# The head of an attention and feed-forward kernel: key copies from separate PSUM tiles, an earlier values' matrix, and two softmax tiles turned by DMA

## The chip, the cores and the metric

The kernel runs on one core of a Trainium2 chip. The time is the device time of the whole program in microseconds (us), the median of three runs. A profile of one execution shows each engine's instructions: TensorE (PE, with its weight loads as PEld), VectorE (DVE), ScalarE (ACT), GpSimd (POOL) and the queue of SyncE (SP), which here only issues DMAs.

## The reference

Attention in which each block of 96 positions looks at one sorted block, and behind it a gated feed-forward layer. 4 batches, 8 heads, 768 positions of 64 elements, 8 blocks a head; 3072 tokens of 512 elements go through w_in (512 x 2048) and w_out (2048 x 512).

```python
P = sort_net                                  # (4, 8, 8, 8)
for _ in range(5):                            # Sinkhorn
    P = exp(P - P.max(-1)); P = P / (P.sum(-1) + 1e-9); P = P / (P.sum(-2) + 1e-9)
k_sorted = einsum('bhij,bhjcd->bhicd', P, k in blocks)
v_sorted = einsum('bhij,bhjcd->bhicd', P, v in blocks)
scores = q_block @ k_sorted_block.T / sqrt(64)      # 96 x 96 per block and head
attn = softmax(scores)
x = (attn @ v_sorted_block), heads side by side     # (3072, 512)
h = x @ w_in
out = (h * cos(h)) @ w_out
```

## The kernel before

The tokens are done in eight chunks n = 0 to 7 of 384 tokens: chunk n is batch n // 2 and four of its eight blocks. A unit u = 0 to 3 of a chunk is one block with its eight heads. Within each engine the instructions run in the order in which the program text issues them (it is written out by hand, lines 900 to 1221); engines wait for each other through semaphores that the framework derives from the tiles that are read and written. Two engines that use the same bank of one PSUM tile are put one after the other by it. PSUM has two pools: `big`, three tiles of two banks, called B in the hand-written order, and `acc`, two tiles of one bank, called C.

The head is what comes before the feed-forward products of chunk 0. Its steps:

- `sort_net` (8 KB) is loaded on SP's queue. POOL issues all other loads: queries, keys and values of batch 0, the four parts of w_in, the queries of chunk 1, the four parts of w_out, and later the next batch. POOL's loads go through one DMA queue (q0 in the profile), SP's DMAs through another (q1).
- VectorE sets constants and zeros (lines 231 to 239), then runs Sinkhorn with ScalarE's exponentials (lines 302 to 376).
- `block` (line 380) multiplies selection matrices with the sorted P; `spread` (line 391), on VectorE, puts the result on the diagonal blocks of `bds[0]` (keys) or `bdv` (values).
- `kp` (line 744) multiplies 16 slices of the keys with the block matrix into a PSUM tile of two banks; `k_place` copies half the blocks of such a tile to kT, the first half (half 0) for chunk 0, the second for chunk 1. There are three such tiles, 0, 1 and 2, and the copies are shared between VectorE (V) and ScalarE (A).
- POOL permutes half of the values (`v_permute`, line 169); `v0` (line 774) multiplies eight slices of the values with bdv; `v0e` copies them to vS on ScalarE. vS has a column of ones per block, set by `ones` on POOL, so that the product with it gives the softmax's sums.
- For each unit of chunk 0, in the order 0, 3, 1, 2: `s_ps` (line 791) makes the scores; `s_max` and `s_sub` on VectorE take the maximum and subtract it; `expo` (line 565) makes the exponential on ScalarE into one of three buffers p_buf, 96 x 8 x 128 with 32 columns of padding a head; the tile is turned to pT; `av_products` multiplies it with vS, `av_norm` divides on VectorE; `x_ps` turns the result on TensorE and `x_ev` copies it to xT.
- The turning has two ways. With `on_pe` true, `p_ps` transposes the eight heads on TensorE into PSUM and `p_ev` copies them to pT on VectorE or ScalarE. Otherwise `expo` itself issues a DMA transpose of the whole p_buf, padding included, on SP's queue (line 588). In the head all four units are turned on TensorE; from chunk 2 on most are turned by DMA. The buffer of unit 0 is used again by the fourth exponential, that of unit 2.
- `keep_warm` (line 244) issues products of a tile of zeros whose result is overwritten. In the head there are ten between the scores and the av products, through the argument `fill`.
- From `up_four` on (line 850) the products with w_in and w_out follow, with the work of chunk 1 between them. `z_vperm`, `z_turned` and `p_pads` are POOL's zeros; `p_pads` sets the padding of the three p_bufs for the DMA transposes of the later chunks.

Of the kernel before, what the change touches and what calls it, by code (L numbers as in the profile page):

```python
# [10 lines left out]
FP32 = mybir.dt.float32  # L11
# [7 lines left out]
def kernel(  # L19
# [15 lines left out]
    nc = tc.nc  # L35
    B, H, S, D = q.shape
    nb = sort_net.shape[-1]
    blk = S // nb
# [9 lines left out]
    IC = 4  # L48
# [5 lines left out]
    NB = H2 * nb  # L54
# [40 lines left out]
    vS = {}  # L95
# [107 lines left out]
    PB = H * nb  # L203
# [5 lines left out]
    pick, pick_pair = pick_at(0, 2), pick_at(2, 2)  # L209
# [16 lines left out]
    def ones(g):  # L226
        nc.gpsimd.memset(vS[g][:, :, D:D + 1], 1.0)
# [10 lines left out]
    nc.vector.memset(nones[:], 0.0)  # L238
    zero_words(nc.vector, vperm[64:, CD - 12 * blk:CD])

    early = const.tile([128, 1], FP32, name="early")
    nc.scalar.activation(early[:], half_pi[:], AF.Exp)

    def keep_warm(times, t, cols=512):
        for _ in range(times):
            nc.tensor.matmul(
                t[:, :cols], warm[:], warm[:, :1].to_broadcast([128, cols]),
                start=True, stop=True)
# [131 lines left out]
    def block(picked, pool=acc, tag="acc"):  # L380

        ps = pool.tile([128, nb], FP32, name="bl", tag=tag)
        for z, part in enumerate(picked):
            n = part.shape[2]
            for j in range(nb):
                nc.tensor.matmul(
                    ps[z * n:(z + 1) * n], part[:, j], sorted_by[:, :, j],
                    start=(j == 0), stop=(j == nb - 1))
        return ps

    def spread(dst, ps, rows=slice(0, 128), xs=slice(0, 2 * H)):
        shape = [rows.stop - rows.start, xs.stop - xs.start, nb]
        nc.vector.tensor_tensor(
            dst[rows, xs], maskp[rows, xs].to_broadcast(shape),
            ps[rows].unsqueeze(1).to_broadcast(shape), op=ALU.mult)

    blocks = [block([pick[:]])]
    spread(bds[0], blocks[0], xs=slice(H, 2 * H))

    def values_matrix():  # L400
        spread(bdv, blocks[1], xs=slice(0, H))
        spread(bds[0], blocks[0], xs=slice(0, H))
        spread(bdv, blocks[1], xs=slice(H, 2 * H))

    MH = H2 * IC

    def k_products(ps, t, c, rows, rhs, keys=kbuf):
        nc.tensor.matmul(  # L408
            ps[:, t], keys[rows, c * 2 * D:(c + 1) * 2 * D], rhs, start=True, stop=True)
# [155 lines left out]
    def expo(n, u, on_pe=False):  # L565
        p = p_bufs[cnt[0] % NP]
        cnt[0] += 1


        nc.scalar.activation(  # L570
            p[:, :, :blk], s_t.pop((n, u)).rearrange("p e h c -> p (e h) c"), AF.Exp,
            scale=scale)
        if u == 0 and n in (NQ, NQ + 1):

            w = 2 * H2 * blk
            c = 2 * (QZ + D) + (n - NQ) * w
            t = kbuf[:, c:c + w].rearrange("p (a c) -> p a c", c=blk)
        elif n < LATE:
            t = ptp.tile([128, 2 * H2, blk], BF16, name="pT", tag="pT")
        else:  # L580

            z, w = (n * IC + u) % 8, 2 * H2 * blk
            t = vperm[:, z * w:(z + 1) * w].rearrange("p (a c) -> p a c", c=blk)
        pT[n, u] = t
        if on_pe:
            pb[n, u] = p
        else:
            nc.sync.dma_start_transpose(out=t[:], in_=p.rearrange("p a c -> p (a c)"))
# [25 lines left out]
    def av_products(n, u, fill=0):  # L614
        g, b2, ih = where(n)
        if n not in xT:
            xT[n] = xtp.tile([128, KC, TC], BF16, name="xT", tag="xT")
        a = big.tile([128, 2, 512], FP32, name="av", tag="big")
        keep_warm(fill, a[:, 0], 256)
        pt = pT.pop((n, u)).rearrange("p a c -> p (a c)")  # L620
        for hp in range(2):
            for h2 in range(H2):
                e = hp * H2 + h2
                w = 128 if e < 2 * H2 - 1 else blk
                nc.tensor.matmul(  # L625
                    a[:w, hp, h2 * (D + 1):(h2 + 1) * (D + 1)],
                    pt[:blk, e * blk:e * blk + w],
                    vS[g][:, v_at(g, b2, hp, h2, ih * IC + u), :D + 1],
                    start=True, stop=True)
        av_ps[n, u] = a  # L630
# [104 lines left out]
    def z_vperm():  # L735
        nc.gpsimd.memset(vperm[:64, :VN * blk], 0.0)

    def p_pads():
        for t in p_bufs:
            nc.gpsimd.memset(t[:, :, blk:], 0.0)  # L740

    ps = {}

    def kp(t, pool, tag, fill=0):
        o = ps["k", t] = pool.tile([128, 16, 2 * NB], FP32, name="ks", tag=tag)
        keep_warm(fill, o[:, :8].rearrange("p t n -> p (t n)"))
        for z in range(16):
            k_products(o, z, t * 16 + z, slice(0, 128),
                       bds[0][:, H:].rearrange("p x i -> p (x i)"))

    def k_place(t, eng, half=None):
        lo, hi = (0, nb) if half is None else (half * IC, half * IC + IC)
        o = ps["k", t]
        copy_on(
            eng, kT[0].rearrange("p z (h i) t -> p z h i t", i=nb)[
                :, ::2, :, lo:hi, t * 16:t * 16 + 16],
            o.rearrange("p t (e h i) -> p e h i t", e=2, i=nb)[:, :, :, lo:hi])

    def kxp(t):
# [14 lines left out]
    def v0(z, pool, tag, fill=0):  # L774
        o = ps["v", z] = pool.tile([128, 8, 2 * NB], FP32, name="vs", tag=tag)
        keep_warm(fill, o.rearrange("p t n -> p (t n)"))
        for t in range(8):

            d = z * 8 + t
            w = 1 if d >= VN else min(8 - t, 2)  # L780
            m = blk if d >= VN and t == 7 else 128
            nc.tensor.matmul(  # L782
                o[:m, t:t + w].rearrange("p w n -> p (w n)"), v_cols(d, d >= VN, m),
                bdv[:, :H].rearrange("p x i -> p (x i)").unsqueeze(1).to_broadcast(
                    [128, w, 2 * NB]), start=True, stop=True)
# [5 lines left out]
    def s_ps(n, u, fill=0):  # L791
        o = ps["s", n, u] = big.tile([128, 2, 512], FP32, name="sc", tag="big")
        keep_warm(fill, o[:, 0])
        if n == 0:
            for a in range(2 * H2):
                hp, c = a // H2, (u * H2 + a % H2) * blk
                for x in range(2):
                    rows = slice(x * D, (x + 1) * D)
                    m, w = a % H2 * nb + u, HT if a % H2 == H2 - 1 else 64
                    keys = kT[0][rows, 2 * hp].rearrange("p m t -> p (m t)")  # L800
                    nc.tensor.matmul(
                        o[:, x, a * HT:a * HT + w], q_of(0, hp)[rows, c:c + 128],
                        keys[:, m * HT:m * HT + w], start=True, stop=True)
            return
        if u < 2:
            by_half(n, u, o)
            return
        for h2 in range(H2):
            for hp in range(2):
                scores(o[:, hp, h2 * 128:h2 * 128 + blk], n, u, h2, hp)  # L810
# [86 lines left out]
    def w_next(eng=A, pool=None, tag="acc"):  # L897
        v_sort_g(next(wz), 4, eng, pool or acc, tag)

    kp(2, *B)  # L900
    kp(0, *B)
    v_permute(slice(0, 64), 32, False, 8, 40)
    v_permute(slice(0, 64), 40, False, 8, 48)
    v_permute(slice(0, 64), 48, False, 8, 56)
    v_permute(slice(0, 64), 56, False, 8, 64)
    k_place(2, A, 1)
    k_place(2, V, 0)
    kp(1, *B)
    k_place(0, A, 0)
    blocks.append(block([pick[:, :, z * PB:(z + 1) * PB] for z in (1, 0)]))  # L910
    k_place(1, V, 0)
    k_place(1, A, 1)
    values_matrix()
    k_place(0, A, 1)
    s_ps(0, 0, fill=3)
    v0(4, *C)
    s_max(0, 0)
    v0(0, *B)
    v0e(4, A)
# [9 lines left out]
    load_w_out(2)  # L929
    load_w_out(3)  # L930
    v0(6, *C)
    ones(0)
    expo(0, 0, True)
    s_ps(0, 2)
    s_sub(0, 3)
    v0(1, *C)
    v0e(6, A)
    s_max(0, 1)
    expo(0, 3, True)
    v0(3, *B, fill=2)  # L940
    s_sub(0, 1)
    v0e(1, A)
    p_ps(0, 0, *C, fill=2)
    v0e(3, A)
    s_max(0, 2)
    v0(7, *C)
    expo(0, 1, True)
    kxp(2)
    v0(2, *B, fill=1)
    p_ev(0, 0, V)  # L950
    v0e(7, A)
    s_sub(0, 2)
    kxp(0)
    p_ps(0, 1, *C)
    v0e(2, A)
    p_ps(0, 3, *C)
    p_ev(0, 1, V)
    expo(0, 2, True)
    kxp(1)
# [1 line left out]
    z_turned(1)  # L961
    av_norm(0, 0, True)
    av_products(0, 1)
    p_ev(0, 3, A)
    p_ps(0, 2, *C)
    av_norm(0, 1, True)
    x_ps(0, 0, *B)
# [1 line left out]
    p_ev(0, 2, A)  # L969
    load(vbuf, 64, vin_d[1])  # L970
    picks(pick_pair, (2, 3))
    av_products(0, 3, fill=2)
    av_norm(0, 3, True)
    x_ps(0, 1, *C)
    x_ev(0, 0, A)
# [12 lines left out]
    up_four(0, 3, 1)  # L988
    z_turned(0)
    cos_four(0, 0)  # L990
    p_pads()
    up_four(0, 1, 0)
    cos_four(0, 3)
    gate_four(0, 0)
# [256 lines left out]
```

## Time and profile before

| | |
|---|---|
| runs | 232.80, 232.88, 232.88 us; median 232.88 |
| profiled execution, first to last instruction | 231.6 us |
| TensorE busy | 223.5 us, 97% |
| VectorE, ScalarE, POOL busy | 170.9, 154.2 and 95.9 us |
| first product with w_in (line 857) | starts at 27.86 us |

The profile's own time is the span; the difference to the runs' median lies before the first and after the last instruction. A line of a timeline or a group names the start and the time in us, the engine, the line of the program, the operation, output<-inputs by tile name, the shapes, the count, and in brackets the idle time before it with the engine that ended it. Where a helper issues the instruction the line is the helper's: line 257 is every copy on ScalarE, 259 every copy on VectorE. A row of a DMA queue gives packets, megabytes and the packets' time as a share of 16 engines; a row of DMA issues gives their count, size and the median time from issue to landing.

### The profile page before, as it was taken

What the parts mean: (1) busy time and instruction counts of PE and PEld (TensorE: products, weight loads), DVE (VectorE), ACT (ScalarE), POOL (GpSimd) and SP (SyncE); (2) the same over time, 40 slices, a digit from 0 to 9 for tenths busy, and PEclk for the clock granted to TensorE, in tenths of its full rate; (3) what the DMA queues carried; (4) which work ended last, traced back from release to release, by engine and by line L of the source; (5) the groups of instructions that cost most, each with busy time, mean ns of one, the idle gap of its engine ahead of it and who ended that gap; (6) DMA issues with size and microseconds to landing.
All of it is one profiled execution on the core that took longest, in us unless ns stands there. A gap on an engine that the chain in (4) does not pass through costs nothing.

```text
span 231.6 us, 5534 instructions
## 1 busy us (share of the span) xinstructions
PE 223.5 (97%) x2268; PEld 138.9 (60%) x2268; DVE 170.9 (74%) x291; ACT 154.2 (67%) x207; POOL 95.9 (41%) x121
## 2 busy tenths in 40 slices
PE   8888999999999999999999999999999999999994
PEld 3477898567665566644666456555655566556553
DVE  6769968978789778877389986997699769745700
ACT  5658877777789858794888566746675666716521
POOL 7999999399950188932709000900000000000000
PEclk9999999999999999999999999999999999999999
DMA  5999999994999999797989839964923450351012
GB/s 69 230 191 207 202 207 233 199 225 139 125 135 172 174 137 148 130 168 158 154 138 89 122 72 146 215 90 92 207 91 69 90 167 0 68 146 45 0 45 93
DMA packets 67673, 31.21 MB, mean 135 GB/s; under 512 B 56384, under 2 KB 63168, under 8 KB 67392
## 3 DMA queue, kind: packets, MB, share of 16 engines
q0 software_dynamic: 24048, 13.64, 43.5%
q1 hardware_dynamic: 43312, 17.02, 35.1%
q8 instruction: 18, 0.29, 0.5%
q10 hardware_dynamic: 288, 0.20, 0.3%
q14 instruction: 7, 0.06, 0.1%
HBM read 27.27 MB, written 6.29 MB: 145 GB/s over the span
## 4 chain that ended last, share of the span: by engine, by line
PE 85%; DMA 5%; DVE 3%; POOL 2%; ACT 2%; issue 1%; SPq 1%; POOLq 0%; ACTq 0%
PE h L669 30%; PE o L694 28%; PE h L857 5%; PE o L878 5%; DMA kTs<-kTs 4%; PE av L625 3%; PE sc L438 3%; PE ks L408 2%; PE o L1215 2%; PE pps L835 1%; PE xps L656 1%; PE sc L504 1%; PE vs L782 1%; PE xps L844 1%; SPq L421 1%
## 5 line engine op out<-in xcount | busy, mean ns | idle before, releaser
L669 PE MATMUL h<-xT,w_in_t 128*128 128x384 bf16 x448 | 78.4, 326 | 0.0
L694 PE MATMUL o<-w_out_t,gg 128*128 128x512 bf16 x320 | 76.2, 379 | 0.0
L677 DVE TENSOR_TENSOR gg<-c,h 128x768 bf16<-128x768 f32 x56 | 52.7, 949 | 20.0 <-ACT c L673 20.0
L673 ACT ACTIVATE c<-h,half_pi 128x768 f32<-128x768 f32 x56 | 50.4, 900 | 25.3 <-PE h L669 24.4
L669 PEld LDWEIGHTS <-w_in_t 128*128 128x128 bf16 x448 | 42.2, 98 | 26.5 <-DMA xT<-xn 0.4
L694 PEld LDWEIGHTS <-gg 128*128 128x128 bf16 x320 | 28.9, 98 | 28.4
L179 POOL COPY vperm<-kv 64x768 bf16<-64x768 bf16 (+2 forms) x12 | 28.4, 2413 | 3.9 <-DMA kv<-in_v_dram 3.9
L570 ACT ACTIVATE p_buf<-s 96x768 bf16<-96x768 f32 x32 | 26.6, 842 | 5.1 <-DVE s L491 4.0
L489 DVE TENSOR_REDUCE mx<-sc 96x4 f32<-96x384 f32 (+1 forms) x33 | 24.0, 728 | 2.2 <-PE sc L504 2.2
L491 DVE TENSOR_TENSOR s<-sc,mx 96x384 f32<-96x384 f32 (+1 forms) x33 | 24.3, 735 | 1.6
L638 DVE TENSOR_TENSOR xn<-av,r 96x512 bf16<-96x512 f32 x32 | 22.0, 686 | 1.1
L129 POOL DMA_DIRECT2D kv<-in_q_dram x24 | 16.0, 680 | 0.8 <-issue 0.5
L257 ACT COPY kv<-o 128x512 f32<-128x512 f32 (+2 forms) x10 | 5.2, 523 | 14.1 <-PE o L694 11.5
L257 ACT CAST kTs<-ks 128x512 bf16<-128x512 f32 (+1 forms) x18 | 11.0, 630 | 5.3 <-PE ks L408 4.4
L636 DVE RECIPROCAL r<-av 96x8 f32<-96x8 f32 x32 | 6.4, 199 | 7.9 <-PE av L625 7.6
L878 PE MATMUL o<-w_out_t,gg 128*128 128x512 bf16 x48 | 11.7, 379 | 0.0
L438 PE MATMUL sc<-kTs,q_turned 128*128 128x96 bf16 x152 | 11.0, 206 | 0.5 <-DMA kTs<-kTs 0.5
L129 POOL DMA_DIRECT2D q_mem<-in_q_dram x16 | 10.7, 690 | 1.8 <-DMA kv<-in_v_dram 1.5
L259 DVE COPY kv<-o 128x512 f32<-128x512 f32 (+1 forms) x5 | 3.1, 612 | 11.1 <-PE o L1215 8.5
L857 PE MATMUL h<-xT,w_in_t 128*128 128x192 bf16 x128 | 11.1, 246 | 0.0
L438 PEld LDWEIGHTS <-q_turned 128*128 128x128 bf16 x152 | 8.8, 98 | 3.0 <-issue 0.6
L857 PEld LDWEIGHTS <-w_in_t 128*128 128x128 bf16 x128 | 10.5, 98 | 0.0
(134 smaller groups left out, 279.1 us busy)
## 6 DMA issues: line engine op xcount, KB each, us to landing
out_dram<-kv SPq DMA_DIRECT2D x12, 256.0 KB, 2.6
out_dram<-o_s SPq DMA_DIRECT2D x10, 256.0 KB, 3.1
w_in_t<-in_moe_w_in_dram POOLq DMA_DIRECT2D x4, 512.0 KB, 11.8
w_out_t<-in_moe_w_out_dram POOLq DMA_DIRECT2D x4, 512.0 KB, 12.4
kv<-in_k_dram POOLq DMA_DIRECT2D x2, 768.0 KB, 9.9
kv<-in_v_dram POOLq DMA_DIRECT2D x2, 768.0 KB, 13.0
pair<-in_k_dram POOLq DMA_DIRECT2D x2, 768.0 KB, 12.4
kv<-in_v_dram POOLq DMA_DIRECT2D x6, 256.0 KB, 5.7
```

The source lines that it names most:

```text
L129: nc.gpsimd.dma_start(out=q_heads[:, i, :, e], in_=src[:, ih * IC + i, :, e])
L179: nc.gpsimd.tensor_copy(dst, src)
L438: nc.tensor.matmul(out, q_of(n, hp)[:, x:x + 128], keys_of(n, u, h2, hp), start=True, stop=True)
L489: nc.vector.reduce_max(mx[:], scv, axis=AX.X)
L491: nc.vector.tensor_tensor(s, scv, mx.to_broadcast(list(s.shape)), op=ALU.subtract)
L570: nc.scalar.activation(p[:, :, :blk], s_t.pop((n, u)).rearrange("p e h c -> p (e h) c"), AF.Exp, scale=scale)
L669: nc.tensor.matmul(h[:, f2, :w], w_in_t[:, kk, f * 128:(f + 1) * 128], xT[n][:, kk], start=(kk == 0), stop=(kk == KC - 1))
L673: nc.scalar.activation(c[:], h[:, :, :w], AF.Sin, bias=half_pi[:, 0:1])
L677: nc.vector.tensor_tensor(gt[n, fp // 2][:, f:f + 2], c[:], h[:, :, :w], op=ALU.mult)
L694: nc.tensor.matmul(o[:], gt[n, f // 4][:, f % 4, ts * 128:(ts + 1) * 128], w_out_t[:, f, :], start=(f == 0), stop=(f == FC - 1))
L857: nc.tensor.matmul(o[:, part, f2 * w:(f2 + 1) * w], w_in_t[:, kk, f * 128:(f + 1) * 128], xT[0][:, kk, h * w:(h + 1) * w], start=(kk == 0) ...
L878: nc.tensor.matmul(out_ps[ts][:], gt[0, q][:, f % 4, ts * 128:(ts + 1) * 128], w_out_t[:, f, :], start=(f == 0), stop=(f == FC - 1))
```

## The change

- VectorE sets the padding of the p_bufs among its first zeros; `p_pads` is gone from POOL.
- The block product of the values stands right behind that of the keys, ahead of the key products; the four spreads stand together, and the column of ones of vS[0] is set by VectorE behind them, no longer by POOL.
- `kp` takes the first slice, the number of slices, and the pool: slices 32 to 47 and 0 to 15 in tiles of `big`, 16 to 23 and 24 to 31 in two tiles of `acc`. The copies are: 32 first half VectorE, 0 first half ScalarE, 16 both halves VectorE, 24 both halves ScalarE; the second halves of 0 and 32 follow on ScalarE behind the first scores and the first value products.
- Units 0 and 3 are turned by the DMA transpose that `expo` issues; their `p_ps` and `p_ev` are gone. Units 1 and 2 stay on TensorE.
- The ten products of zeros are gone.

```diff
+    for t in p_bufs:
+        nc.vector.memset(t[:, :, blk:], 0.0)
...
-    blocks = [block([pick[:]])]
+    blocks = [block([pick[:]]), block([pick[:, :, z * PB:(z + 1) * PB] for z in (1, 0)])]
     spread(bds[0], blocks[0], xs=slice(H, 2 * H))
-
-    def values_matrix():
-        spread(bdv, blocks[1], xs=slice(0, H))
-        spread(bds[0], blocks[0], xs=slice(0, H))
-        spread(bdv, blocks[1], xs=slice(H, 2 * H))
+    spread(bdv, blocks[1], xs=slice(0, H))
+    spread(bds[0], blocks[0], xs=slice(0, H))
+    spread(bdv, blocks[1], xs=slice(H, 2 * H))
+    nc.vector.memset(vS[0][:, :, D:D + 1], 1.0)
...
-    def p_pads():
-        for t in p_bufs:
-            nc.gpsimd.memset(t[:, :, blk:], 0.0)
...
-    def kp(t, pool, tag, fill=0):
-        o = ps["k", t] = pool.tile([128, 16, 2 * NB], FP32, name="ks", tag=tag)
-        keep_warm(fill, o[:, :8].rearrange("p t n -> p (t n)"))
-        for z in range(16):
-            k_products(o, z, t * 16 + z, slice(0, 128),
+    def kp(c, n, pool, tag):
+        o = ps["k", c] = pool.tile([128, n, 2 * NB], FP32, name="ks", tag=tag)
+        for z in range(n):
+            k_products(o, z, c + z, slice(0, 128),
                        bds[0][:, H:].rearrange("p x i -> p (x i)"))
...
-    kp(2, *B)
-    kp(0, *B)
+    kp(32, 16, *B)
+    kp(0, 16, *B)
+    kp(16, 8, *C)
+    kp(24, 8, *C)
     v_permute(slice(0, 64), 32, False, 8, 40)
...
-    k_place(2, A, 1)
-    k_place(2, V, 0)
-    kp(1, *B)
+    k_place(32, V, 0)
     k_place(0, A, 0)
-    blocks.append(block([pick[:, :, z * PB:(z + 1) * PB] for z in (1, 0)]))
-    k_place(1, V, 0)
-    k_place(1, A, 1)
-    values_matrix()
+    k_place(16, V, 0)
+    k_place(24, A, 0)
+    k_place(16, V, 1)
+    k_place(24, A, 1)
+    s_ps(0, 0)
+    v0(4, *C)
     k_place(0, A, 1)
-    s_ps(0, 0, fill=3)
-    v0(4, *C)
+    k_place(32, A, 1)
     s_max(0, 0)
...
-    ones(0)
-    expo(0, 0, True)
+    expo(0, 0)
...
-    expo(0, 3, True)
-    v0(3, *B, fill=2)
+    expo(0, 3)
+    v0(3, *B)
...
-    p_ps(0, 0, *C, fill=2)
...
-    v0(2, *B, fill=1)
-    p_ev(0, 0, V)
+    v0(2, *B)
...
-    p_ps(0, 3, *C)
...
-    p_ev(0, 3, A)
...
-    av_products(0, 3, fill=2)
+    av_products(0, 3)
...
-    p_pads()
```

More of the change, by code (lines that the diff above doesn't have):

```diff
@@ L736, in z_vperm, with k_place @@
         nc.gpsimd.memset(vperm[:64, :VN * blk], 0.0)
-    def p_pads():
-        for t in p_bufs:
-            nc.gpsimd.memset(t[:, :, blk:], 0.0)
     ps = {}
-    def kp(t, pool, tag, fill=0):
-        o = ps["k", t] = pool.tile([128, 16, 2 * NB], FP32, name="ks", tag=tag)
-        keep_warm(fill, o[:, :8].rearrange("p t n -> p (t n)"))
-        for z in range(16):
-            k_products(o, z, t * 16 + z, slice(0, 128),
+    def kp(c, n, pool, tag):
+        o = ps["k", c] = pool.tile([128, n, 2 * NB], FP32, name="ks", tag=tag)
+        for z in range(n):
+            k_products(o, z, c + z, slice(0, 128),
                        bds[0][:, H:].rearrange("p x i -> p (x i)"))
-    def k_place(t, eng, half=None):
-        lo, hi = (0, nb) if half is None else (half * IC, half * IC + IC)
-        o = ps["k", t]
+    def k_place(c, eng, half):
+        lo, hi = half * IC, half * IC + IC
+        o = ps["k", c]
         copy_on(
             eng, kT[0].rearrange("p z (h i) t -> p z h i t", i=nb)[
-                :, ::2, :, lo:hi, t * 16:t * 16 + 16],
+                :, ::2, :, lo:hi, c:c + o.shape[1]],
             o.rearrange("p t (e h i) -> p e h i t", e=2, i=nb)[:, :, :, lo:hi])
```

## The prediction

> **What bounds the kernel now.** I read the page first, then the chain of waits, then the stretches by window. From the page: the span, the engines' busy time, and the DMA engines' busy tenths in 40 slices.
>
> ```profile
> span 231.6 us, 5534 instructions
> PE 223.5 (97%) x2268; PEld 138.9 (60%) x2268; DVE 170.9 (74%) x291; ACT 154.2 (67%) x207; POOL 95.9 (41%) x121
> DMA  5999999994999999797989839964923450351012
> ```
>
> TensorE is busy for 223.5 of 231.6 us, so the time is what TensorE must do plus the holes in its row. The chain of waits (start, length, what) shows where the holes are:
>
> ```profile
> 12.25 0.37 PE bl L386 x8
> ...
> 12.91 1.56 PE ks L408 x48
> 14.47 0.51 PE bl L386 x16
> 14.98 0.77 PE sc L246 x3
> 15.75 0.35 PE sc L801 x16
> ...
> 28.03 3.30 PE h L857 x40
> ```
>
> Until 28 us the chain jumps between engines; from the first matmul with w_in (L857, 28.03) it is nearly all TensorE. A window after that has no hole:
>
> ```profile
> 32.00:40.00 8.00, 8.00 (x122) 7.54 (x120) 6.29 (x10) 5.54 (x7) 7.83 (x11) 1.00 1.17 221
> ```
>
> The first and second numbers behind the window are its length and TensorE's busy time; they are equal, the clock is 1.00, and the second number from the end is the share of the 16 DMA engines in use: over 1. So **whatever the head gains or loses until the first L857 goes into the total one for one**, and the DMA engines have no spare time meanwhile. A moved start of L857 is what I have to find; it is 27.86 us before. The trace's 231.6 us span lies 1.3 us under the runs' median of 232.88; I add my difference to 232.88.
>
> **Part 1: the key copies and the values' matrix.** The rows of ScalarE and VectorE around the copies:
>
> ```profile
> 13.57 1.07 ACT L257 CAST kTs<-ks 128x512 bf16<-128x512 f32 x2 [1.60 <-PE ks L408]
> 14.19 1.29 DVE L259 CAST kTs<-ks 128x512 bf16<-128x512 f32 x2 [1.33 <-ACT kTs L257]
> 15.51 1.07 ACT L257 CAST kTs<-ks 128x512 bf16<-128x512 f32 x2 [0.87 <-DVE kTs L259]
> 15.68 0.40 PE L801 MATMUL sc<-kTs,q_turned 64*128 64x64 bf16 x16
> 16.12 0.95 DVE L821 TENSOR_REDUCE mx<-sc 96x8 f32<-96x768 f32 x1 [0.25 <-PE sc L801]
> ```
>
> The two engines take turns on one PSUM tile: VectorE idles 1.33 us for ScalarE, then ScalarE 0.87 us for VectorE. The first scores need the first halves of all copies, the last of which ends at 14.19 + 1.29 = 15.48; the three products of zeros (0.77 in the chain) lie in that wait and end after it, so the scores start at 15.68. With four tiles, each read by one engine at a time, neither waits for the other. The values' block now stands ahead of the key products: 0.51 us, of which 0.29 lies in TensorE's wait for the first spread (12.91 - 12.25 - 0.37), so the products, which end at 14.47, move by 0.2 us to about 14.7. ScalarE's copy of the last tile, of 256 columns, costs between half and all of 0.54 us (1.07 / 2); I take 0.4 and get 15.1 for the last first half, 15.2 for the scores: **0.5 us earlier**. The added spreads and the memset of the ones' column (under 0.2 us by the rows below) lie in VectorE's 1.33 us of idleness; without that cover they would cost 0.2. The second halves are late instead, behind the first scores; what waits for them is the fourth scores' last columns and the reuse of a PSUM tile by the values, and the values wait for POOL anyway.
>
> The pads of the three p_bufs move from POOL's later work to VectorE's first instructions:
>
> ```profile
> 0.99 0.48 DVE L232 MEMSET pair<- 32x512 uint32 x1
> 1.46 0.09 DVE L236 MEMSET q_turned<- 128x32 uint32 x1
> ...
> 2.30 0.07 DVE L303 MEMSET Q<- 32x8 f32 x1
> 2.47 0.21 DVE L304 TENSOR_REDUCE top<-P 32x8 f32<-32x64 f32 x1
> ```
>
> A pad has 8 x 32 bf16, 128 words a row, between the 32 words of 0.09 us and the 512 of 0.48: about 0.17 each, 0.5 for three, less some overlap of starts. VectorE is free only from 2.37 to 2.47, and Sinkhorn's first reduction stands behind them. Bounds 0 and 0.5; I take **0.3 us later**, which all of Sinkhorn passes on. Net at the first maximum: 0.2 us earlier.
>
> **Part 2: what leaves the engines.** VectorE's eviction of the first turned tile stands between a maximum and its subtraction:
>
> ```profile
> 21.70 0.93 DVE L821 TENSOR_REDUCE mx<-sc 96x8 f32<-96x768 f32 x1
> 22.56 0.54 DVE L259 COPY pT<-pps 96x768 bf16<-96x768 bf16 x1
> 23.02 0.94 DVE L825 TENSOR_TENSOR s<-sc,mx 96x768 f32<-96x768 f32 x1
> ```
>
> Without it the subtraction could start at 22.68 instead of 23.02: 0.34 us. ScalarE loses one eviction, TensorE two groups of eight transposes and ten products of zeros. These fill TensorE's holes and are off the path, but for 0.1 or 0.2 us. Together (0.2, 0.34 and 0.15) the first av products could come about 0.7 us earlier, and so could L857, **if the turned tiles are there**. POOL sheds four memsets; nothing on the path asks for that time.
>
> **Part 3: two tiles turned by DMA.** SP now issues a transpose behind expo(0,0) and behind expo(0,3). Their ends, and TensorE's use of the tiles:
>
> ```profile
> 18.35 0.84 ACT L570 ACTIVATE p_buf<-s 96x768 bf16<-96x768 f32 x1
> 19.99 0.85 ACT L570 ACTIVATE p_buf<-s 96x768 bf16<-96x768 f32 x1
> 24.33 0.88 PE L625 MATMUL av<-vS,pT 96*128 96x65 bf16 x16
> 26.18 0.42 PE L625 MATMUL av<-vS,pT 96*128 96x65 bf16 x8
> 27.86 0.25 PE L857 MATMUL h<-xT,w_in_t 128*128 128x192 bf16 x1
> ```
>
> The exponentials end at 19.19 and 20.84; ScalarE has three value copies before the first, which wait for POOL's permutations, so I move them by only 0.2: issues at 19.0 and 20.6. The tiles are needed for av(0,0), at 24.33 or up to 0.9 earlier, and for av(0,3), the row at 26.18. Behind av(0,0) on TensorE stands everything else. Behind the first landing stands also expo(0,2), the fourth user of three p_bufs: ScalarE waits there, with the evictions and xT copies queued behind it.
>
> A transpose with little company costs 2.8 us from issue to landing, as from 128 to 135 us:
>
> ```profile
> q1 hardware_dynamic: 2816, 0.69, 53.5%
> ...
> pT<-p_buf SPq DMA_TRANSPOSE x3, 2.8
> ```
>
> (packets, MB, share of the 16 engines). But from 16 to 28 us the loads' queue q0 fills the engines:
>
> ```profile
> q0 software_dynamic: 2824, 2.42, 126.7%
> ```
>
> What SP's queue q1 gets beside a full q0 is seen at 82 us, where a p_buf's transpose is issued behind loads:
>
> ```profile
> 81.97 1.45 SPq L588 DMA_TRANSPOSE kv<-p_buf  x1
> ```
>
> From 82.0 to 86.4 q0 is the only queue with packets, though the transpose has been issued:
>
> ```profile
> q0 software_dynamic: 374, 0.70, 99.0%
> ...
> kv<-p_buf SPq DMA_TRANSPOSE x1, 8.3
> ```
>
> Not one packet of q1 for 4.4 us, and 8.3 to the landing. From 86.5 to 88.5 the two share packet by packet:
>
> ```profile
> q0 software_dynamic: 785, 0.13, 85.5%
> q1 hardware_dynamic: 661, 0.17, 67.0%
> ```
>
> and from 49.5 to 52.5, where stores are issued into full pair loads, they do the same:
>
> ```profile
> q0 software_dynamic: 96, 0.56, 89.8%
> q1 hardware_dynamic: 93, 0.19, 18.5%
> ```
>
> So two terms. **The first packet**: between 1.2 us (the issue itself) and 4.5; the loads of the head have smaller packets (2.42 MB / 2824 = 860 bytes) than those at 82 (0.70 / 374 = 1,870), so I take 3.5. **The share**: a p_buf is 96 x 1024 x 2 = 196,608 bytes, in packets of 0.69 MB / 2816 = 245, nominally 256: 768, or 48 per engine. One packet of q0 takes 12 us x 16 / 2824 = 0.068 us of an engine, one of q1 0.535 x 7 us x 16 / 2816 = 0.021. One for one: 48 x 0.089 = 4.3 us a tile; bounds 3.3 (q1's own time free) and 5. The first tile lands at 19.0 + 3.5 + 4.3 = 26.8, the second, behind it in the same queue, at **31.1**. The lower bounds give 23.5 and 26.8, the upper ones 28.5 and 33.5.
>
> av(0,3) thus moves from 26.18 to 31.1, and from it to L857 the order is as before (1.68 us; the same norm and the same x_ps). L857 at 32.8 against 27.86: **4.9 us later**. The gains of Parts 1 and 2 end in that wait. Sum: 232.88 + 4.9 = 237.8; by the bounds 26.8 and 33.5, +0.6 to +7.3.
>
> The Trainium skill, "DMA: Bandwidth & Descriptors", section on queues, rings and completion order, has each engine go round-robin between its queues by packet. The shares above agree; the silent 4.4 us do not. By that rule the first packet would come with the issue, and the estimate would be 28.8 for the second tile, so 235.5 in all, inside the likeliest case's own range below.
>
> **The rivals.** (a) *The transposes stay hidden.* At 2.8 us they land at 21.8 and 23.4, before use, and the gain of 0.7 us stands: **232.2**. For it: transposes with little company do take 2.8. Against it: q0's 126.7% all through, and the samples at 82 and 49 us. It decides as soon as the second lands before about 25.5. (b) *A soon first packet, q1's packets nearly free*: the lower bounds, second tile at 25.8 to 27.5: **233.5**, from the same time to 1.3 us slower. The loads' smaller packets speak for it. (c) *The wait, and the clock with it.* TensorE would stand idle from about 23.5 to 26.8 and again before 31; without products of zeros nothing fills that. The trace shows what a lower clock costs:
>
> ```profile
> 1.00 5.90 PE L246 MATMUL idle<-warm 128*128 128x512 bf16 x14 [1.00 <-DVE warm L231]
> 14.94 0.81 PE L246 MATMUL sc<-warm 128*128 128x512 bf16 x3
> ```
>
> 14 of 512 columns in 5.90 us at the start are 0.42 each, three later ones at 0.22 apart: half pace for over 5 us. That again around L857 costs 1.7 to 2.8 us: **240.2**. Against it: no idle stretch in the trace ahead of L857 is long enough to show a drop. The Trainium skill, "TensorE: Matmul & The Clock Gate", on why this matters, allows no gap over some 3 us between bursts; by it the first gap is a borderline case, and no row of before shows one. (d) *The copies still take turns*, and Part 1's 0.5 us is not there: hidden in the DMA wait, the time stays 237.8; under (a) it is 232.7.
>
> **How the numbers follow.** The DMA wait with a full clock 0.50, 237.8, its own range 234.5 to 240.2; (c) 0.20; (b) 0.13; (a) 0.15; (d) changes none of them; 0.02 for what I don't see. No change means within 0.2%, 0.47 us, about what a measurement of this kernel can tell. Faster: (a) and a little of (b), 0.16; same 0.07; slower 0.77. The range runs from the edge of (a), 232.2, to 241.0, past the middle of (c); it leaves out most of (a) and the end of (c).
>
> **What would show it.** Right: av L625 waits for a DMA into pT twice, the second past 29 us; q1 gets about as many packets as q0 while it runs; expo(0,2) waits for the first landing; L857 starts near 33; windows after that look as before. Part 1 is right if VectorE and ScalarE copy keys with no wait for each other and the first scores start before 15.6. Wrong: landings under 5 us after their issue, or L857 before 28.5; a clock under 1.00 from 24 to 40 us makes it (c).

## The result, and the profile after

The changed kernel takes **243.19 us** (four executions, 241.66 to 247.53) against 232.88 for the kernel before: ratio 1.0401, 95% interval 1.0351 to 1.0451, **slower by 9.3 us (8.2 to 10.5)**. The forecast was 237.8, range 232.2 to 241.0: the sign was right, the size was outside the range. The comparisons leave out disturbed executions: the longest of the four above is one, and e3's profiled one below, of which no row is shown for that reason. The profiled execution took 242.67 us.

The page after, its span, busy times, granted clock and DMA rows in 40 slices:

```profile
span 240.8 us, 5490 instructions
...
PE 224.4 (93%) x2242; PEld 139.9 (58%) x2242; DVE 171.6 (71%) x295; ACT 153.6 (64%) x207; POOL 94.5 (39%) x117
...
PEclk9999758999999999999999999999999999999999
DMA  6999999699199969989797997975671670152012
```

TensorE is busy for almost the same time as before (224.4 us against 223.5) in a span 9.2 us longer, so the time went into idleness and into slow products, and the clock row says where: slices 5 to 7, 24 to 42 us. TensorE's row there (start, length, instructions, and in brackets the idle time ahead and what ended it):

```profile
22.77 0.56 PE L832 MATMUL pps<-ident,p_buf 96*96 96x96 bf16 x8
28.07 1.11 PE L627 MATMUL av<-vS,pT 96*128 96x65 bf16 x16 [4.75 <-DMA pT<-p_buf]
29.01 0.87 PE L832 MATMUL pps<-ident,p_buf 96*96 96x96 bf16 x8
...
32.36 0.65 PE L627 MATMUL av<-vS,pT 96*128 96x65 bf16 x8 [2.12 <-DMA pT<-p_buf]
...
34.82 4.72 PE L854 MATMUL h<-xT,w_in_t 128*128 128x192 bf16 x40
```

TensorE waits for the two transposes, 4.75 and 2.12 us, and reaches its first product with w_in (L854, L857 before) at 34.82 instead of 27.86. Then it is also slow: forty of these products, 3.47 us each time they are seen at full clock below, take 4.72. On ScalarE the fourth exponential hangs on the first landing:

```profile
28.11 0.84 ACT L572 ACTIVATE p_buf<-s 96x768 bf16<-96x768 f32 x1 [4.44 <-DMA pT<-p_buf]
```

Stretches of 3.41 us, the unit in which the granted clock changes in every trace of this case (second number: TensorE's busy time; third from the end: its clock):

```profile
23.75:27.16 3.41, 0.00 (x0) 0.00 (x0) 0.17 (x1) 0.00 (x0) 3.23 (x6) 1.00 1.38 172
27.16:30.57 3.41, 2.17 (x28) 1.94 (x28) 1.69 (x4) 1.50 (x2) 3.26 (x7) 0.50 1.26 186
30.57:33.99 3.42, 1.63 (x28) 1.57 (x29) 0.91 (x3) 1.00 (x3) 3.42 (x3) 0.50 1.24 201
33.99:37.40 3.41, 3.41 (x37) 3.15 (x33) 1.69 (x4) 2.08 (x2) 3.30 (x5) 0.50 1.24 208
37.40:40.81 3.41, 3.41 (x46) 3.41 (x44) 1.91 (x3) 2.20 (x3) 0.02 (x1) 1.00 1.24 241
```

Behind a stretch in which TensorE does nothing, the clock is half; it stays half behind two stretches with 2.17 and 1.63 us of work, and is full again behind one that was filled. The Trainium skill, "TensorE: Matmul & The Clock Gate", Part 1, describes just this: a free-running window of about 3.4 us, half clock after an idle one, full after a busy one. This trace agrees, to the window; that of e1, in the last section, does not, where the clock fell behind a stretch with 2.50 us of work. Behind the two waits stand three windows at half clock, 10.24 us in all.

The transposes' queue (SP's issues; then q0 and q1 from 19.0 to 22.6 us and from 24 to 32: packets, MB, share of 16 engines):

```profile
18.98 3.75 SPq L590 DMA_TRANSPOSE pT<-p_buf  x2
...
q0 software_dynamic: 739, 0.74, 123.4%
q8 instruction: 1, 0.02, 1.7%
...
q0 software_dynamic: 1456, 1.11, 89.8%
q1 hardware_dynamic: 1414, 0.35, 36.6%
```

From 19.0 to 22.6 us q1 has not one packet, though the first transpose was issued at 18.98; its first ten come between 22.8 and 23.0, some 3.9 us behind that issue. From 24 to 32 us it has one for each of q0's.

Part 1 shows in these rows, VectorE's and ScalarE's key copies and the first scores:

```profile
2.32 0.45 DVE L242 MEMSET p_buf<- 96x128 uint32 x3
...
14.05 0.89 DVE L262 CAST kTs<-ks 128x512 bf16<-128x512 f32 x1 [0.20 <-PE ks L410]
14.87 0.73 DVE L262 CAST kTs<-ks 128x256 bf16<-128x256 f32 x2
14.40 2.12 ACT L260 CAST kTs<-ks 128x512 bf16<-128x512 f32 x5 [2.21 <-PE ks L410]
15.33 0.40 PE L798 MATMUL sc<-kTs,q_turned 64*128 64x64 bf16 x16 [0.50 <-DVE kTs L262]
```

No copy waits for the other engine any more, and the first scores start at 15.33 instead of 15.68.

### The profile page after: what moved, and what is told of

It reads as the page before. It is cut to its first block, busy times and chain, and to the rows that moved or that the text cites. A ratio compares the mean times of both kernels' runs of the same rounds, so it can differ in the third digit from the quotient of the medians.

```text
span 240.8 us, 5490 instructions
## 1 busy us (share of the span) xinstructions
PE 224.4 (93%) x2242; PEld 139.9 (58%) x2242; DVE 171.6 (71%) x295; ACT 153.6 (64%) x207; POOL 94.5 (39%) x117
## 4 chain that ended last, share of the span: by engine, by line
PE 78%; DMA 11%; DVE 3%; issue 2%; ACT 2%; POOL 2%; ACTq 0%; POOLq 0%
PE h L671 30%; PE o L696 22%; DMA pT<-p_buf 9%; PE h L854 5%; PE o L875 4%; PE av L627 3%; PE sc L440 2%; PE ks L410 2%; DMA vperm<-p_buf 2%; PE o L1207 1%; PE xps L658 1%; PE qps L271 1%; ACT p_buf L572 1%; ACT L572 1%; PE vs L451 1%
## 5 line engine op out<-in xcount | busy, mean ns | idle before, releaser
L679 DVE TENSOR_TENSOR gg<-c,h 128x768 bf16<-128x768 f32 x56 | 52.7, 949 | 20.2 <-ACT c L675 20.2
L671 PEld LDWEIGHTS <-w_in_t 128*128 128x128 bf16 x448 | 42.3, 98 | 26.3 <-DVE xT L262 0.3
L627 PE MATMUL av<-vS,pT 96*128 96x65 bf16 x120 | 7.1, 209 | 7.7 <-DMA pT<-p_buf 7.7
L260 ACT CAST kTs<-ks 128x512 bf16<-128x512 f32 (+2 forms) x19 | 11.0, 610 | 5.0 <-PE ks L410 5.0
L627 PEld LDWEIGHTS <-pT 96*128 96x128 bf16 (+1 forms) x144 | 7.2, 109 | 11.0 <-DMA pT<-p_buf 9.3
L854 PE MATMUL h<-xT,w_in_t 128*128 128x192 bf16 x128 | 12.3, 261 | 0.0
L854 PEld LDWEIGHTS <-w_in_t 128*128 128x128 bf16 x128 | 11.6, 105 | 0.2
## 6 DMA issues: line engine op xcount, KB each, us to landing
w_in_t<-in_moe_w_in_dram POOLq DMA_DIRECT2D x4, 512.0 KB, 11.5
```

Source lines behind the costliest of these rows:

```text
L627: nc.tensor.matmul(a[:w, hp, h2 * (D + 1):(h2 + 1) * (D + 1)], pt[:blk, e * blk:e * blk + w], vS[g][:, v_at(g, b2, hp, h2, ih * IC + u), : ...
L671: nc.tensor.matmul(h[:, f2, :w], w_in_t[:, kk, f * 128:(f + 1) * 128], xT[n][:, kk], start=(kk == 0), stop=(kk == KC - 1))
L679: nc.vector.tensor_tensor(gt[n, fp // 2][:, f:f + 2], c[:], h[:, :, :w], op=ALU.mult)
L854: nc.tensor.matmul(o[:, part, f2 * w:(f2 + 1) * w], w_in_t[:, kk, f * 128:(f + 1) * 128], xT[0][:, kk, h * w:(h + 1) * w], start=(kk == 0) ...
```

## The experiments

The theory: the loss is the late landing of two tiles behind the loads' queue, and the half clock that the idle TensorE gets for it. Rivals: the other parts of the change (no products of zeros, pads on VectorE, order of the key copies) lose part of it; or a DMA transpose is slow whatever runs beside it.

### Which part: e1_pe_turned and e2_dma_only

e1 is the changed kernel with units 0 and 3 turned on TensorE again:

```diff
-    expo(0, 0)
+    expo(0, 0, True)
...
-    expo(0, 3)
+    expo(0, 3, True)
...
+    p_ps(0, 0, *C)
...
+    p_ev(0, 0, V)
...
+    p_ps(0, 3, *C)
...
+    p_ev(0, 3, A)
```

> The changed kernel with units 0 and 3 turned on TensorE again (transposes and evictions at their old places), all else as changed, no products of zeros. Theory (the DMA landings cause the loss, the lower clock follows from the wait): no wait for a DMA in the head, clock 1.00 throughout, first product with w_in at about 27.3 us, total 232.2 to 232.9. Rival 1 (the missing products of zeros let the clock fall by themselves): clock under 1.00 somewhere between 20 and 40 us, total 234.5 or more. Rival 2 (key copies, values' block or the early padding cost the time): total stays above 240.

Measured: 233.13 against 233.21 (ratio 1.0006, 0.9991 to 1.002). The loss is gone, but the 232.2 to 232.9 of the theory was missed, and so was its full clock: one stretch ran at half clock (last section). That is the sign of rival 1, without its 234.5.

e2 is the mate, the kernel before with only the turning of these two units moved to DMA, and the pads that these transposes read set by VectorE as in the change:

```diff
+    for t in p_bufs:
+        nc.vector.memset(t[:, :, blk:], 0.0)
...
-    expo(0, 0, True)
+    expo(0, 0)
...
-    expo(0, 3, True)
+    expo(0, 3)
...
-    p_ps(0, 0, *C, fill=2)
...
-    p_ev(0, 0, V)
...
-    p_ps(0, 3, *C)
...
-    av_products(0, 0)
+    av_products(0, 0, fill=2)
...
-    p_ev(0, 3, A)
...
-    p_pads()
```

> The kernel before with the two tiles of units 0 and 3 turned by DMA and the pads of the p_bufs on VectorE: key copies, values' block and eight of the ten products of zeros stay as before, two stand ahead of av(0,0). If the transposes alone make the change, landings are 27.5 to 28.5 and 31.8 to 32.8, the clock falls behind the first wait, and the time is 240.5 to 243.5, like the changed kernel's. If the other parts of the change lose time or the lost products of zeros make the clock fall, it is 239 to 240.3, as where the waits were filled.

Measured: 242.70, ratio 1.0411 (1.0385 to 1.0437). Its TensorE row:

```profile
28.28 1.11 PE L628 MATMUL av<-vS,pT 96*128 96x65 bf16 x16 [4.49 <-DMA pT<-p_buf]
...
33.48 0.65 PE L628 MATMUL av<-vS,pT 96*128 96x65 bf16 x8 [2.61 <-DMA pT<-p_buf]
```

The second tile came later than expected, at 33.48. The two tiles make the whole loss, with ten products of zeros in the head (e2 keeps them, two moved ahead of av(0,0)) or with none; everything else in the change is worth nothing that can be measured.

### One tile at a time: e5_only_unit0 and e6_only_unit3

The changed kernel with only one of the two edits of e1 left undone: unit 0 by DMA and unit 3 on TensorE (e5), or the reverse (e6).

> The changed kernel with unit 3's tile turned on TensorE again and unit 0's by DMA: the mate of the kernel that turned unit 3 alone, 7.1 us slower than before. If a landing sets the end through the place of its av products, unit 0's tile lands at 27.5 to 28.5, av(0,0) waits 4.3 to 4.8 us, the clock falls to half for 3.4 or 6.8 us, and the first product with w_in starts at 31.2 to 32.2: 237.5 to 239.5 in all, less than unit 3 alone. If the two tiles' costs add, 236 (10 less 7.1).

> The changed kernel with unit 0 turned on TensorE again, unit 3 alone by DMA. Theory (a silent time of about 3.9 us behind queued loads, then one packet of the transpose to one of the loads, 50 turns, 4.3 to 5 us): issue at 20.6 to 20.9, landing 8 to 9 us later at about 29.3, av(0,3) waits some 3 us, first product with w_in at 31 to 32, total 235.5 to 238.5 (the upper end if the clock falls). Rival (the second of two is late only because it stands behind the first): landing under 5 us, total 232.5 to 233.5.

Measured: e5 238.72 (1.0244, 1.0211 to 1.0276), e6 240.31 (1.0302, 1.0274 to 1.033). The waits, first of e5, then of e6:

```profile
28.42 1.11 PE L627 MATMUL av<-vS,pT 96*128 96x65 bf16 x16 [3.54 <-DMA pT<-p_buf]
...
32.91 4.33 PE L854 MATMUL h<-xT,w_in_t 128*128 128x192 bf16 x39
```

```profile
30.91 0.65 PE L627 MATMUL av<-vS,pT 96*128 96x65 bf16 x8 [5.32 <-DMA pT<-p_buf]
...
33.37 3.80 PE L854 MATMUL h<-xT,w_in_t 128*128 128x192 bf16 x33
```

Alone they cost 5.7 and 7.0 us by the ratios, together 9.3: they do not add, and I read this as the later landing setting the end. (e5's clock was also half from 21.20 to 24.62 us, ahead of its wait, which was shorter for it: 3.54 us for 4.75.) Unit 3's tile took 10.0 us with no transpose ahead of it in its queue, hardly less than its 11.5 behind unit 0's; I expected a landing near 29.3. Being second costs little; being behind q0 costs nearly all.

### Is it the loads' queue? e4_queue_free, e4b_q_early, e4c_tight

e4 holds two quarters of w_in, the queries of chunk 1 and all of w_out back until the transposes are issued, so that q0 is empty at 20 us:

```diff
-            for z in ((0, 1, 2), (3,))[it // 2]:
+            for z in ((0, 3), ())[it // 2]:
                 load_w_in(z)
...
-    load_q(1)
...
-    load_w_out(0)
...
     z_turned(1)
+    load_q(1)
+    for z in (1, 2):
+        load_w_in(z)
+    for z in range(4):
+        load_w_out(z)
```

> The changed kernel with POOL's loads held back: only parts 0 and 3 of w_in are loaded early; the queries of chunk 1, parts 1 and 2 of w_in and all of w_out are issued behind z_turned(1), at about 25 us, so the loads' queue runs empty at about 20 us. Theory (the transposes wait behind queued loads): both land within 4.5 us of their issue, the first before 23.7, the second before 25.5, no wait of av over 0.7 us, clock 1.00, first product with w_in before 28; total 231.5 to 236, since loads that are later now may be waited for. Rival (a transpose of a padded p_buf is slow in itself here, whatever the queue holds): landings still 8 us or more after issue and a total above 240.

Measured: 241.28, ratio 1.0352 (1.0318 to 1.0386); expected were 231.5 to 236. The queues from 19 to 20 and from 20 to 24 us, and the transposes' landing (issues, median us):

```profile
q0 software_dynamic: 4, 0.00, 2.0%
...
q1 hardware_dynamic: 1600, 0.39, 74.8%
...
pT<-p_buf SPq DMA_TRANSPOSE x2, 3.3
```

and TensorE:

```profile
23.72 0.68 PE L625 MATMUL av<-vS,pT 96*128 96x65 bf16 x16 [0.40 <-ACT vS L260]
...
31.03 0.86 PE L271 MATMUL qps<-ident,q_mem 96*64 96x96 bf16 x16 [4.44 <-DMA q_mem<-in_q_dram]
```

The first half of the expectation came in full: 3.3 us instead of over 9, no wait for a tile. The total did not, by an error of mine: the queries that I held back are needed at 27 us, and landed at 31; behind that wait the clock was half, from 27.84 to 34.67. So a transpose is not slow by itself; the queue makes it so.

e4b keeps `load_q(1)` early and issues the two quarters of w_in ahead of `z_turned(1)`; only w_out and those two are held.

> The changed kernel with only the loads that nobody waits for soon moved behind the transposes: w_in quarters 1 and 2 stand behind kxp(1), the four of w_out behind z_turned(1); quarters 0 and 3 and load_q(1) keep their early places. If the loads' queue is what makes the transposes late, and the whole loss hangs on that: landings within 5 us of their issue (first by 24.2, second by 25.5), no wait of av products for a DMA over 0.5 us, no half clock between 26 and 37 us, the first L854 product (here L852) between 26.9 and 28.0, and 231.9 to 233.6 in all, so 9 to 11 us less than the changed kernel. If the missing products of zeros lose time by themselves, the clock shows 0.50 somewhere from 20 to 40 us and the time is 233.5 to 236 with the same landings. If a transpose by DMA is slow whatever stands beside it, landings of 8 us and more and over 238.

Measured: 238.31 (237.75 in the profiled execution), ratio 1.0187 (1.0138 to 1.0236): about 5 us better than the changed kernel, 4 worse than before, where 231.9 to 233.6 was expected. Landings after 3.7 us (median of two). Its rows:

```profile
23.74 0.67 PE L627 MATMUL av<-vS,pT 96*128 96x65 bf16 x16 [0.40 <-ACT vS L260]
...
26.21 0.66 PE L627 MATMUL av<-vS,pT 96*128 96x65 bf16 x8
...
27.90 4.29 PE L854 MATMUL h<-xT,w_in_t 128*128 128x192 bf16 x40
...
46.47 0.41 PE L410 MATMUL ks<-bd,kv 128*128 128x64 bf16 x8 [1.85 <-DMA kv<-in_k_dram]
```

```profile
24.00:26.00 2.00, 1.57 (x33) 1.23 (x29) 1.73 (x5) 1.35 (x3) 1.96 (x2) 1.00 0.88 111
26.00:28.00 2.00, 1.98 (x33) 1.80 (x34) 1.65 (x4) 1.01 (x3) 1.96 (x5) 0.54 1.24 198
```

With the tiles in time the head is as long as before (27.90 against 27.86), not shorter. The last av products are still 0.64 us ahead (26.21; 26.85 before), but the clock falls at 26.2 us with no long gap ahead of it: from there to L854 TensorE takes 1.69 us for 1.01, and the forty products another 0.8 more (4.29 for 3.47). Then comes the price of an empty queue: the next batch's keys, loaded behind the held loads, are 1.85 us late. The remaining 1.5 of the 4.2 us in the span (235.8 against 231.6) is added later and was not traced. The share of DMA engines in use, 0.88 here, is 1.38 in the changed kernel's stretch from 23.75.

e4c moves one part of w_out ahead again and puts thirteen products of zeros between 15 and 26 us.

> The kernel with the held loads and an early load_q(1), with w_out's first quarter moved ahead of z_turned(1) and thirteen products of zeros put into the stretch from 15 to 26 us. If the rest of the loss there is one window at half clock (1.2 us) and the loads' queue standing empty until its k half was 1.85 us late, the clock is 1.00 throughout, the wait of the ks products for kv is under 1.0 us, the first product with w_in starts between 27.2 and 27.9, and the time is 232.8 to 234.8. If the clock falls all the same, 235 or more; if the wait for kv stays at 1.8, 234.8 to 236.

Measured: 238.24 as the median of four, 236.24 and 236.54 in the two compared, ratio 1.0145 (1.0117 to 1.0172). The wait for the keys went down to 0.81 us as expected; the clock fell all the same, at 19.0 us, and the first product with w_in came at 28.84. That is the case in which 235 or more was expected. No version with DMA transposes in the head came nearer to the kernel before than these 3.4 us.

### What the clock costs, and what a delay alone costs: e3_warm and e13

e3 fills the two waits with products of zeros:

```diff
-    av_products(0, 0)
+    av_products(0, 0, fill=42)
...
-    av_products(0, 3)
+    av_products(0, 3, fill=18)
```

> The changed kernel with 42 products of zeros of 256 columns ahead of av(0,0) and 18 ahead of av(0,3), so that TensorE works while it waits for the two landings. Theory: the landings stay at 28.0 and 32.3 us, the clock stays 1.00, the first product with w_in comes at about 34.1 instead of 34.8 and the feed-forward behind it is no longer stretched by 1.25, so 2.0 us less than the changed kernel: 240.5 to 241.5. If the lower clock were not part of the loss: 243.

Measured: 239.85, ratio 1.0289 (1.0267 to 1.0311), the clock 0.998 to 1.0 in the executions compared: 2.6 us less than the changed kernel by the two ratios (0.0112 x 233; 1.3 to 3.9 with their intervals), where 2.0 was expected. That the landings stayed where they were no row shows.

e13 leaves DMA transposes out altogether and delays the kernel before by products of zeros ahead of av(0,2), twelve or sixty-five:

```diff
-    av_products(0, 2)
+    av_products(0, 2, fill=65)
```

> The kernel before with twelve more products of zeros of 256 columns ahead of av(0,2): the first product with w_in comes 1.3 us later (27.86 to 29.1), with the clock full, no transposes by DMA and the loads running on. One for one: 1.2 to 1.4 us slower, ratio 1.005 to 1.006. If the part behind has slack of its own (loads that TensorE waits for later), 0.2 to 0.9 us slower.

> The same with sixty-five such products: 7.0 us later, as late as in the changed kernel (34.8), with the clock full. One for one: 239.5 to 240.3, ratio 1.029 to 1.032, and what the changed kernel's 10 us has beyond that is its half clock and its loads. If a delayed head makes later transfers collide by itself, as they seem to in the changed kernel's second half, 240.5 to 242. If the later part has slack, under 239.3.

Measured: 235.15, ratio 1.008 (1.0056 to 1.0104), and 241.28, ratio 1.0349 (1.0322 to 1.0375). TensorE with sixty-five:

```profile
26.72 7.38 PE L246 MATMUL av<-warm 128*128 128x256 bf16 x65
...
34.96 2.23 PE L857 MATMUL h<-xT,w_in_t 128*128 128x192 bf16 x25
...
68.65 0.33 PE L438 MATMUL sc<-kTs,q_turned 128*128 128x96 bf16 x4 [1.45 <-DMA kTs<-kTs]
```

With the start of L857 where the changed kernel has it (34.96 against 34.82), at full clock and with no transpose, 7.1 us of delay make 7.9 of loss. So about 8 of the 9.3 us can be had by the delay alone, and it grows on its way: the wait at 68.65 was 0.47 us before. The shorter delay, 1.2 us at L857 (29.06), made 1.9 (1.3 to 2.4). Why a later start makes that later wait longer the runs don't tell.

### Where the gains of the head went: e8 to e12

Five kernels without DMA transposes in the head. e8 is e1 with the pads back on POOL; e9 is e8 with the ten products of zeros of before; e10 is the kernel before with these taken out; e11 is e8 with

```diff
-            for z in ((0, 1, 2), (3,))[it // 2]:
+            for z in ((0, 1, 2), ())[it // 2]:
                 load_w_in(z)
...
     load_q(1)
+    load_w_in(3)
```

and e12 is e11 with the products of zeros.

> All tiles turned on TensorE, no products of zeros, and the pads of the p_bufs back on POOL behind the head: the key copies and the values' block are the only parts of the change left, with the fills gone. If the pads on VectorE cost Sinkhorn 0.3 us that the whole head passes on, the bl products start at 12.25 instead of 12.47, and the time is 0.2 to 0.4 under the 233.1 of the kernel that differs in the pads alone: 232.7 to 232.9. If the cost of the pads is hidden behind a later wait, 233.0 to 233.2.

> As the one before, with the kernel before's ten products of zeros back in their places: only the key copies from four tiles and the early values' block are left of the change. If these products hold the clock, it is 1.00 from 7 us to the end in every execution, and the gain of 0.4 to 0.6 us at the first scores reaches the end: 232.2 to 232.6, ratio under 0.999. If the products of zeros are only weight in TensorE's row, this is 0.1 to 0.3 slower than the kernel without them. If the head's gain ends in a later wait (the values' permutations on POOL), it equals the kernel before: 232.7 to 233.1.

> The kernel before with its ten products of zeros taken out and nothing else changed. If they hold the clock where the head has holes, some window of 3.4 us between 15 and 30 us shows 0.50 and the time is 0.2 to 0.8 above the kernel before: 233.1 to 233.7. If they are only weight, 0.1 to 0.3 below it: 232.6 to 232.8, with a clock of 1.00 throughout.

> The kernel with the key copies and the values' block alone (no products of zeros, pads on POOL), with load_q(1) issued ahead of the last quarter of w_in instead of behind it. There TensorE reached av(0,0) 0.62 us earlier than in the kernel before and lost 0.48 of it at 27.07 to q_mem's landing. If this landing is what swallows the head's gain, q_mem lands near 24.5, the wait at the qps products is gone, the first L855 product starts at 27.2 to 27.4 (before 27.86), and the time is 0.4 to 0.7 us under the kernel before: ratio 0.9970 to 0.9985. If another wait stands right behind (w_in's last quarter, the fourth xps), L855 stays at 27.6 or later and the ratio is 0.999 to 1.001.

> The kernel with the key copies, the values' block and load_q(1) ahead of w_in's last quarter, now with the ten products of zeros of before in their places. Without them its first product with w_in came at 26.82, 1.04 us earlier than before, and yet twelve runs gave the time of before. If the start of that product goes into the time one for one and the missing products of zeros gave the gain away in some runs, it is 0.5 to 0.9 us under before: ratio 0.996 to 0.998. If a later wait for loads takes the gain of the head, whatever the head does, the ratio is 0.999 to 1.001 again.

Measured, ratio to before: e8 1.0016 (0.9992 to 1.004), e9 0.9999 (0.9978 to 1.002), e10 1.0014 (0.9988 to 1.004), e11 1.0001 (0.9987 to 1.0014), e12 1.0001 (0.998 to 1.0022). Not one differs from the kernel before, though the heads do; the gains that were expected of e9, e11 and e12 did not come, nor a full clock in every execution of e9. TensorE in e8:

```profile
15.10 0.40 PE L799 MATMUL sc<-kTs,q_turned 64*128 64x64 bf16 x16 [0.50 <-DVE kTs L259]
...
23.71 0.88 PE L624 MATMUL av<-vS,pT 96*128 96x65 bf16 x16
...
27.07 0.56 PE L268 MATMUL qps<-ident,q_mem 96*64 96x96 bf16 x16 [0.48 <-DMA q_mem<-in_q_dram]
...
27.75 3.47 PE L855 MATMUL h<-xT,w_in_t 128*128 128x192 bf16 x40
```

and in e11:

```profile
23.34 0.99 PE L625 MATMUL av<-vS,pT 96*128 96x65 bf16 x16
...
26.15 0.56 PE L268 MATMUL qps<-ident,q_mem 96*64 96x96 bf16 x16
...
26.82 3.47 PE L856 MATMUL h<-xT,w_in_t 128*128 128x192 bf16 x40
```

e8 is 0.62 us ahead at av(0,0) (before: 24.33) and 0.11 ahead at the first product with w_in: between them stand the queries of chunk 1, for whose load TensorE waits until 27.07. The pads' price can be read at the first scores, 15.10 against 15.33 in the changed kernel. e11 takes that wait away and is 1.04 ahead, in the profiled execution to the end (232.02, the shortest of its twelve). Over the twelve runs nothing is left of it.

Spans and clocks of the single runs show a part of where it went. In e8 the nine executions with a mean clock of 0.999 or more have spans of 231.07 us on average, against 231.51 of the kernel before beside them, and the three others, at 0.991 to 0.993, have 232.2 to 233.0. And in 7 of the 46 executions of e1, e8, e10 and e11, which have no products of zeros in the head, the time lies 2.5 to 3.0 us above the span; in e9, e12 and the kernel before beside them it stays within 2.0, and the runs don't tell why. In e11, where no execution is under 0.998, the spans are still only 0.2 us shorter than before (231.03 for 231.24). Where the rest of its 1.04 us goes stays open, and so does the reading by which a gain passes through one for one.

The products of zeros weigh something in single traces (e12 reaches L856 at 27.60, e11 at 26.82) and nothing in the times. Nor do they decide on the clock by themselves: the mean granted clock was under 0.996 in 2 of 12 runs of e10, 9 of 46 of the four kernels without them (e1, e8, e10, e11) and 4 of 24 of e9 and e12, which have them. The 75 runs of the kernel before beside these never fell under 0.997.

## Why the prediction was wrong in size

By its own steps:

- **Part 1** was right in mechanism and near in size: first scores 0.35 us earlier at 15.33 (0.2 net was taken, "before 15.6" named as its mark), the pads 0.45 us long, which made Sinkhorn's first reduction 0.25 us later (0.3 was taken), no turns between the engines. Rival (d) is out.
- **Part 2** said that the first av products could come about 0.7 us earlier "and so could L857". The first half holds where the tiles are in time (e4b: 23.74 for 24.33, 0.6 earlier). The second fails in the change's order of loads: `load_q(1)` lands at 27.1 in the trace of before, and the queries' products stand ahead of L857, which e8 could not reach before 27.75. A look at that landing would have shown it. Rival (a), 232.2, could therefore hardly have come even with tiles in time. e4b does not test this: its queries landed at 22.3, and the half clock took its lead.
- **Part 3, the landings.** The mechanism held: a silence, then one packet for one. Both landings were 1.2 us later than forecast, 28.0 and 32.3 for 26.8 and 31.1, by three small terms, which add up for the second tile. The silence was 3.9 us (taken: 3.5). The 1,600 packets of the two tiles came from 22.9 to 32.0 us, 9.1 us instead of 8.6: 50 for each engine and tile (1600 / 2 / 16) and not 48, and 0.091 us a pair instead of 0.089. The landing came 0.3 us behind the last packet, for which nothing was taken. (The shares of q0 and q1 from 24 to 32 us add up to 126%, so the times of their packets overlap and must not be added for a pair.) The rule of the Trainium skill, "DMA: Bandwidth & Descriptors", section on queues, rings and completion order, was weighed there: each engine goes round-robin between its queues by packet. The shares agree again, 1,414 packets for 1,456; a silence it does not have, and here one lasted 3.9 us while q0 was full. With an empty q0 (e4) q1's first packets came between 20.2 and 20.4 us, 1.2 to 1.4 behind the issue at 18.99.
- **How the numbers follow: the step that failed most.** The likeliest case, 0.50, had the clock stay full, because "no idle stretch in the trace ahead of L857 is long enough to show a drop". The forecast itself put one of some 3.3 us there and another behind it, and the clock was half from 27.16 to 37.40 us; rival (c), 0.20, was the case that came. Its price of 1.7 to 2.8 us was right: 0.78 between the second landing and L854 (2.46 us for 1.68) and 1.25 in the forty products of L854 (4.72 for 3.47).
- **One for one.** The time of a late L857 was taken as its delay. It was more: 1.1 us is added behind 60 us in the changed kernel, and e13's 7.1 made 7.9 with no half clock at all. The cause of this part is open.

The sum with what was measured: 4.9 + 1.2 (landing) + 0.8 + 1.25 (clock) + 1.1 (later waits) = 9.25 us, for the span's 9.2 (240.8 - 231.6). The executions lie 1.9 us above their span after, 1.3 before on that chip; in the later sessions the kernel before lies 1.7 to 2.0 above its own, so the 0.6 between can't be put down to the change.

## What to carry to other kernels

A transfer that replaces work on an engine has to be priced at its place: time the queues at the moment of its issue, since a DMA transpose of 3 us took 9 to 11.5 behind loads that filled the engines, and emptying that queue only made other loads late. If the forecast itself puts TensorE idle for a whole window of 3.4 us, the half clock behind it belongs into the likeliest case and not into a rival. And before a gain in a head is carried to the end, look for the next load that TensorE waits for: here it stood 0.1 us behind.

## What was not expected of the hardware

A clock can fall with no long gap: in e1 it was 0.50 from 20.03 to 23.44 us behind a stretch in which TensorE was busy for 2.50 of 3.41 us, with no idle time over 0.73 in it:

```profile
16.62:20.03 3.41, 2.50 (x72) 2.07 (x72) 3.34 (x5) 2.81 (x6) 3.41 (x4) 1.00 1.23 203
20.03:23.44 3.41, 3.41 (x41) 3.38 (x40) 3.38 (x5) 3.12 (x6) 3.33 (x6) 0.50 1.24 205
23.44:26.86 3.42, 2.99 (x64) 2.65 (x63) 2.92 (x8) 3.23 (x6) 3.20 (x7) 1.00 1.36 202
```

The changed kernel has the same stretch with 2.50 us busy and keeps its clock there. The busy time of a stretch does not decide it alone: the clock also fell behind 2.12 us (e5, at 21.20, with one gap of 1.29 us), 2.44 (e4c, at 19.04) and 2.56 (e4b, at 26.18), and stayed full behind 1.66 (e4, at 10.77). What tips it isn't settled by these runs; in e1's time (ratio 1.0006) it can't be seen.
